# Making x by VectorE block transposes and on-chip DMAs, and a denser preparation of batch 0, in a fused clustered-attention and snake-MLP kernel

## The chip, the cores and the metric

One core of one Trainium2 chip. The time is the device time of one execution in microseconds; a kernel's time is the median of several executions. The first three executions of the kernel before agree within 0.4%. A profile is one execution recorded instruction by instruction; its span (317.6 us before) is a little shorter than that execution's time (319.34 us).

## The reference, cut to what matters

```python
# q, k, v: (4 batches, 8 heads, 768, 64); centroids: (8 heads, 16 clusters, 64)
q_assign = argmax(q_n @ c_n.T); k_assign = argmax(k_n @ c_n.T)
scores = where(q_assign == k_assign, q @ k.T / 8, -1e9)
x = softmax(scores) @ v          # heads side by side: (3072, 512)
h = x @ w_in                     # w_in (512, 2048)
g = h + sin(alpha * h) ** 2 / (alpha + 1e-9)
return g @ w_out                 # w_out (2048, 512)
```

The kernel writes the cluster of each row as a one-hot of 16 beside its 64 dimensions, so that one matmul over 80 rows gives scores that are large only where the clusters agree.

## The kernel before

Two heads are a *pair*, four pairs a batch, sixteen pairs in all. A batch is 48 *attention steps* (12 a pair), then a *hidden phase*: 16 feature blocks through w_in, the snake function and w_out. What the attention phase has left free on TensorE is filled with output products of the batch before. In these traces each engine works in program order (one block transpose of VectorE below waits 14.1 us, and the PV sums behind it wait too), and so does the queue of SP, which issues most DMAs between SBUF tiles. To *issue* a DMA is to hand it over, here some 0.6 us of the issuing queue; it *lands* when its data have arrived. In the listings T is a pair's transposed q and k, QK the same with the one-hot rows below, xs the x of a pair, xq its block-transposed form and xT the transposed x that the hidden phase reads; S, M and OB are areas of PSUM. A step, and the parts that the change touches:

```python
def scores(i):     # TensorE: 768 columns into one of two PSUM areas
    ...
def expo(i):       # ScalarE: exp of the area into pT (bf16)
    ...
def pv(i):         # TensorE: 6 products of 65 columns, summed over 6 steps in the one bank OB
    ...
    if kt == NJ - 1:                       # the sums of one head are done
        nc.vector.reciprocal(out=rec, in_=o3[:, :, D : D + 1])
        nc.vector.tensor_tensor(out=s["xs"][:, :, h, :], in0=o3[:, :, 0:D], ...)

def x_T(m, bk=None):                       # x of pair m, transposed, for the hidden phase
    ...
    for j in range(NJ):
        nc.tensor.transpose(out=xt_ps[:, P * j : P * j + P], in_=xs[:, j, :, :], identity=ident_b)
    nc.vector.tensor_copy(out=xT[:, hp, :], in_=xt_ps[:, 0:S])

def prep_S(m):     # T of q and k for a later pair (from batch 2 on): 8 DMAs, issued by SP
    ...
def prep_asn(m, part=0, parts=1):          # cluster products, 4 f32 matmuls; batch 0: in two halves
    ...
def prep_hot(m, piece, W=HS):              # VectorE: block transpose, max, compare, transpose back
    ...
def prep_move(m):                          # one-hot rows to their place in QK: 4 DMAs, issued by SP
    ...

def hidden_mm(f, ar, k0, k1):              # kk is the pair within the batch
    for kk in range(k0, k1):
        ...
        nc.tensor.matmul(..., rhs=xT[:, kk, lo:hi], ...)
```

At the end of each batch's steps, `hidden_mm(0, A[0], 0, 3)` reads x of the first three pairs; the fourth is always made by `x_T` inside the hidden phase.

The softmax here doesn't subtract the row's maximum and nothing guards it: scores larger than these inputs give would overflow.

## Time and profile before

| | before |
|---|---|
| time, median of 3 | 319.07 us (318.28 to 319.48) |
| first scores of batches 0 to 3 | 11.75, 86.01, 157.93, 229.35 us |
| first hidden product that needs the third pair's x, batches 1 to 3 | 129.2, 200.5, 270.0 us |
| TensorE busy | 97% |

The second and third rows are starts in TensorE's timeline. In the page's 40 slices, each digit is TensorE's busy share in tenths, and in the second line the clock it was granted:

```profile
PE   8789999899999999999999999999999999999995
PEclk9999999999999999999999999999999999999999
```

There is no slice in which TensorE idles for long, so a change can gain mainly by taking instructions from TensorE.

### The profile page before, as it was taken

The numbers are of one execution on the slowest core, as the hardware profiler recorded it, in microseconds if no ns is written. First come the engines' busy times: TensorE is split into PE (matmuls) and PEld (weight loads), VectorE is DVE, ScalarE is ACT, GpSimd is POOL, SyncE is SP. The second block draws the span as 40 slices with busy tenths as digits, with TensorE's granted clock in tenths as the row PEclk, the third lists the DMA queues.
The fourth block names the chain that finished last, engine by engine and source line by source line (L and its number), as shares of the span: only waits on it lengthen the run. The fifth ranks groups of instructions, "written<-read, shape, count | busy, mean of one in ns | idle before, by whom it ended". The sixth has DMA issues, their size and how long they took to land.

```text
span 317.6 us, 7292 instructions
## 1 busy us (share of the span) xinstructions
PE 306.6 (97%) x2835; PEld 183.0 (58%) x2835; DVE 205.3 (65%) x362; ACT 241.3 (76%) x326; POOL 111.3 (35%) x174
## 2 busy tenths in 40 slices
PE   8789999899999999999999999999999999999995
PEld 3456766555556566555556566555556666555544
DVE  4567879577858676587858676587836322577821
ACT  5578979787679888787679888787679999688300
POOL 5857968507603555960004374530001000000000
PEclk9999999999999999999999999999999999999999
DMA  7535899998825656890025656520011000000031
GB/s 232 187 111 164 259 143 207 221 209 215 273 86 124 153 122 153 231 351 32 0 85 131 154 120 141 141 85 0 0 68 42 30 12 35 2 34 0 2 132 66
DMA packets 26242, 37.74 MB, mean 119 GB/s; under 512 B 3856, under 2 KB 20064, under 8 KB 26208
## 3 DMA queue, kind: packets, MB, share of 16 engines
q0 software_dynamic: 8704, 19.93, 24.7%
q1 hardware_dynamic: 17264, 17.30, 20.2%
q8 instruction: 22, 0.36, 0.5%
q14 instruction: 12, 0.10, 0.1%
q10 hardware_dynamic: 240, 0.06, 0.1%
HBM read 27.30 MB, written 6.29 MB: 106 GB/s over the span
## 4 chain that ended last, share of the span: by engine, by line
PE 86%; DVE 7%; ACT 2%; DMA 2%; issue 1%; SPq 0%; DVEq 0%; ACTq 0%
PE M L361 18%; PE S L390 16%; PE S L314 12%; PE OB L329 10%; PE M L390 8%; PE S L315 6%; PE OB L361 5%; PE M L213 4%; PE S L361 2%; DVE gT L410 2%; PE M L143 2%; PE M L353 1%; ACT s_sb L401 1%; DMA q<-in_q_dram 1%; DVE u_sb L408 1%
## 5 line engine op out<-in xcount | busy, mean ns | idle before, releaser
L320 ACT ACTIVATE pT<-S 128x768 bf16<-128x768 f32 x192 | 144.4, 810 | 21.5 <-PE S L315 20.2
L361 PE MATMUL M<-w_out_bf,gT 128*128 128x512 bf16 (+1 forms) x288 | 90.7, 373 | 0.3 <-DVE gT L410 0.3
L314 PE MATMUL S<-QK 80*128 80x512 bf16 x192 | 73.1, 381 | 2.5 <-DMA QK<-ohT 2.4
L390 PEld LDWEIGHTS <-w_in_bf 128*128 128x128 bf16 x512 | 49.6, 98 | 38.0 <-issue 1.8
L329 PEld LDWEIGHTS <-pT 128*128 128x128 bf16 x1152 | 55.8, 97 | 21.5 <-DVE xs L341 0.5
L390 PE MATMUL S<-xT,w_in_bf 128*128 128x512 bf16 x352 | 65.2, 326 | 1.0 <-DVE gT L410 0.8
L329 PE MATMUL OB<-VX,pT 128*128 128x65 bf16 x1152 | 60.7, 193 | 0.3 <-DVE xs L341 0.2
L190 POOL TENSOR_SCALAR QK<-T 64x384 bf16<-64x384 f32 x64 | 33.6, 525 | 69.3 <-DMA T<-Tq 63.3
L401 ACT ACTIVATE s_sb<-S,alpha_col 128x768 bf16<-128x768 f32 x44 | 39.3, 901 | 23.7 <-PE S L390 14.5
L361 PEld LDWEIGHTS <-gT 128*128 128x128 bf16 x400 | 39.0, 97 | 30.7 <-issue 5.5
L315 PE MATMUL S<-QK 80*128 80x256 bf16 x192 | 51.9, 270 | 0.0
L410 DVE SCALAR_TENSOR_TENSOR gT<-u_sb,ralpha,S 128x768 bf16<-128x768 bf16 x44 | 44.5, 1014 | 11.1 <-ACT u_sb L406 8.2
L185 POOL CAST QK<-T 64x768 bf16<-64x768 f32 x32 | 26.4, 825 | 12.9 <-DVE T L149 8.5
L390 PE MATMUL M<-xT,w_in_bf 128*128 128x512 bf16 (+1 forms) x160 | 29.9, 326 | 0.0
L408 DVE TENSOR_TENSOR u_sb<-s_sb 128x768 bf16<-128x768 bf16 x40 | 23.6, 590 | 7.9 <-ACT s_sb L401 7.9
L340 DVE RECIPROCAL rec<-OB 128x6 f32<-128x6 f32 x32 | 6.1, 192 | 34.1 <-PE OB L329 34.1
L315 PEld LDWEIGHTS <-QK 80*128 80x128 bf16 x192 | 18.9, 98 | 15.2 <-issue 1.1
L410 DVE SCALAR_TENSOR_TENSOR gT<-u_sb,ralpha,M 128x512 bf16<-128x512 bf16 (+1 forms) x40 | 22.8, 611 | 6.4 <-ACT u_sb L406 6.0
L401 ACT ACTIVATE s_sb<-M,alpha_col 128x512 bf16<-128x512 f32 (+1 forms) x40 | 20.9, 574 | 7.2 <-PE M L390 7.2
L361 PE MATMUL OB<-w_out_bf,gT 128*128 128x512 bf16 (+1 forms) x80 | 26.2, 358 | 0.0
L202 POOL CAST VX<-v 128x768 bf16<-128x768 f32 x16 | 13.5, 844 | 34.3 <-PE OB L329 33.4
L314 PEld LDWEIGHTS <-QK 80*128 80x128 bf16 x192 | 18.6, 97 | 10.2 <-issue 5.7
(79 smaller groups left out, 270.3 us busy)
## 6 DMA issues: line engine op xcount, KB each, us to landing
T<-Tq SPq DMA_DIRECT2D x64, 96.0 KB, 2.4
out_dram<-o_sb SPq DMA_DIRECT2D x23, 256.0 KB, 2.1
v<-in_v_dram POOLq DMA_DIRECT2D x14, 384.0 KB, 4.6
q<-in_q_dram POOLq DMA_DIRECT2D x13, 384.0 KB, 5.5
k<-in_k_dram POOLq DMA_DIRECT2D x13, 384.0 KB, 6.3
w_in_bf<-in_moe_w_in_dram POOLq DMA_DIRECT2D x4, 512.0 KB, 8.3
w_out_bf<-in_moe_w_out_dram POOLq DMA_DIRECT2D x4, 512.0 KB, 11.4
QK<-ohT SPq DMA_DIRECT2D x60, 24.0 KB, 3.2
```

Of the source, the lines that this page charges most:

```text
L185: nc.gpsimd.tensor_copy(out=QK[0:D, m % NQK, h, :, HS * par : HS * par + HS], in_=src)
L190: nc.gpsimd.tensor_scalar(out=QK[0:D, m % NQK, h, t].rearrange("c (n i a) -> c i n a", i=4, a=32)[:, 2 * par : 2 * par + 2], in0=src[:, t] ...
L202: nc.gpsimd.tensor_copy(out=VX[m % NVX][:, :, :, 0:D], in_=st[m]["v32"])
L314: nc.tensor.matmul(out=dst[:, 0:512], lhsT=lhsT, rhs=T[:, 0, 0:512], start=True, stop=True)
L315: nc.tensor.matmul(out=dst[:, 512:S], lhsT=lhsT, rhs=T[:, 0, 512:S], start=True, stop=True)
L320: nc.scalar.activation(out=pT, in_=area(i)[:, 0:S], func=ACTF.Exp, scale=escale)
L329: nc.tensor.matmul(out=o3[:, j, :], lhsT=pT[:, P * j : P * j + P], rhs=VX[m % NVX][:, h, jof(m // NHP, kt), :], start=(kt == 0 and j == 0) ...
L361: nc.tensor.matmul(out=bk[:, lo:hi], lhsT=gT[:, f, P * mt : P * mt + P], rhs=w_out_bf[:, f, lo:hi], start=(f == 0), stop=(f == NF - 1),)
L390: nc.tensor.matmul(out=ar[lo // 512][:, 0 : hi - lo] if isinstance(ar, tuple) else ar[:, lo:hi], lhsT=lhsT, rhs=xT[:, kk, lo:hi], start=(k ...
L401: nc.scalar.activation(out=s_sb[:, lo:hi], in_=src, func=ACTF.Sin, scale=alpha_col[:, f : f + 1])
L408: nc.vector.tensor_tensor(out=u_sb, in0=s_sb, in1=s_sb, op=ALU.mult)
L410: nc.vector.scalar_tensor_tensor(out=gT[:, f, lo:hi], in0=u_sb[:, lo:hi], scalar=ralpha[:, f : f + 1], in1=src, op0=ALU.mult, op1=ALU.add,)
```

## The change

Its intent is to relieve TensorE in two ways. (1) The x of the first three pairs of batches 1 to 3 is no longer transposed by TensorE. VectorE transposes it in blocks of 32x32, and sixteen DMAs put the blocks in their places. For this xT gets a blocked layout, which TensorE reads in runs of 32 elements. (2) In batch 0 the cluster products are made whole, in steps that have no PV; the one-hots are dense, so the transpose back has 384 columns instead of 768 and the rows take eight DMAs instead of four. Loads and transposes of batch 0 move to other steps.

```diff
+    def x_D(m):
+        s["xq"] = xqp.tile([P, S], BF16, tag="xq", ...)        # a pool of one buffer
+        nc.vector.transpose(out=s["xq"]..., in_=s["xs"].rearrange("p j h (e d) -> p (h e) j d", e=2))
+    def x_S(m):
+        for g in range(4):
+            for i in range(4):
+                nc.sync.dma_start(
+                    out=xT[32 * g : 32 * g + 32, hp, QS * i : QS * i + QS],
+                    in_=st[m]["xq"][32 * i : 32 * i + 32, g, :],
+                )
 ...
-                    rhs=xT[:, kk, lo:hi],
+                    rhs=xT[:, kk, :].rearrange("c (i j a) -> c j i a", i=4, j=NJ)[:, lo // P : hi // P],
 ...
-            at(STEPS * (m + 1) + 4, lambda m=m: x_T(m))
+            if m < NHP:
+                at((16, 29, 43)[m], lambda m=m: x_T(m))
+            else:
+                at(STEPS * (m + 1) + 5, lambda m=m: (x_D(m), x_S(m)))
 ...
+            nc.vector.tensor_tensor(out=s["oh"]..., op=ALU.is_equal)                    # dense, batch 0
+            nc.vector.transpose(out=s["ohT"][:, 0, :], in_=s["oh"])                     # 384 columns
+                for par in range(2):                                                   # in prep_move
+                    nc.sync.dma_start(out=QK[D : D + NHC, m % NQK, h, t, HS * par : HS * par + HS], ...)
 ...
-        (2, ((0, 2), (1, 6), (2, 7), (3, 8)), (11, 12), (7, 10)),
+        (2, ((0, 5), (1, 6), (2, 8), (3, 10)), 14, (7, 11)),
 ...      # the like for pairs 1 to 6; loads, alpha and two transposes of pair 7 moved
```

## The prediction

> **What bounds the kernel now.** I read the page first (busy shares, then the chain that ended last), then TensorE's timeline, then the queue of SP, which issues most of the on-chip transfers.
>
> ```profile
> PE 306.6 (97%) x2835; PEld 183.0 (58%) x2835; DVE 205.3 (65%) x362; ACT 241.3 (76%) x326; POOL 111.3 (35%) x174
> PE 86%; DVE 7%; ACT 2%; DMA 2%; issue 1%; SPq 0%; DVEq 0%; ACTq 0%
> ```
>
> TensorE is the bound: 97% busy and 86% of the chain. SP's queue has 0% of it, so today no issue time costs anything. Four batches follow one another: 48 attention steps (scores, exponential, PV), then a hidden phase of 16 feature blocks. First scores start at 11.75, 86.0, 157.9 and 229.35 us, and the first hidden products at 55.9, 128.68, 199.97 and 269.47 us. An ordinary step in batches 1 to 3 takes 0.73 us from one scores matmul to the next. A step with a transpose of x looks like this in TensorE's timeline:
>
> ```profile
> 102.15 0.38 PE L314 MATMUL S<-QK 80*128 80x512 bf16 x1
> ...
> 102.66 0.50 PE L353 MATMUL M<-ident_b,xs 128*128 128x128 bf16 x6
> 102.99 0.38 PE L361 MATMUL M<-w_out_bf,gT 128*128 128x512 bf16 x1
> 103.20 0.38 PE L314 MATMUL S<-QK 80*128 80x512 bf16 x1
> ```
>
> The six transposes hold TensorE from 102.66 to 102.99: 0.33 us, and the step is 1.05 us long instead of 0.73. That is what the change wants to take away, nine times. Now the queue that will get the work instead, by SP's timeline in batch 1 and by its two lines of code:
>
> ```profile
> 93.07 6.57 SPq L175 DMA_DIRECT2D T<-Tq  x8
> 99.74 0.55 SPq L375 DMA_DIRECT2D out_dram<-o_sb  x1
> 100.39 2.45 SPq L288 DMA_DIRECT2D QK<-ohT  x4
> 103.02 7.02 SPq L175 DMA_DIRECT2D T<-Tq  x8
> 110.14 2.45 SPq L288 DMA_DIRECT2D QK<-ohT  x4
> ```
>
> ```profile
> L288 SPq DMA_DIRECT2D QK<-ohT x60: 507/587/1742, 21.2 to 245.9; - x60
> L175 SPq DMA_DIRECT2D T<-Tq x64: 586/609/2039, 93.1 to 199.0; - x64
> ```
>
> The reader is to see that SP issues one DMA after another, 0.59 to 0.61 us each (0.61 to 0.65 from start to start), almost whatever its size: 24 KB for QK, 96 KB for T. A pair lasts 9.76 us (x transposes at steps 16 and 28), of which SP is already issuing 8 to 9.5 us in batch 1. There is no room for sixteen more.
>
> **What the Trainium skill says.** "DMA: Bandwidth & Descriptors", section "Issuing engines are not separate DMA queues", holds that spreading issues over engines only saves sequencer time, "usually small relative to the DMA itself". The trace agrees only in part: T lands 2.4 us after issue, so the issue of one is a quarter of that, but sixteen issues in a row are four times the landing. "SBUF — State Buffer", "The DMA setup-cost knee", gives every DMA a fixed cost of about 2 us that does not shrink with its size; the 2.4 us for T and 3.2 us for QK agree, so cutting x into 12 KB pieces saves nothing. The same page, "Door 1: The DMA port swizzle", says that reads cost extra only where consecutive accesses leave a 16-byte line; the new reads of x by TensorE are runs of 32 bf16, 64 bytes, so I give them no cost. No read of such a kind is in this trace. "TensorE: Matmul & The Clock Gate", "Part 1: The HAM clock gate", has TensorE at half clock after some 3.4 us of idleness, until it has been busy as long. The trace before shows full clock nearly throughout, since nothing idles so long.
>
> **The change, part by part.**
> *x by VectorE and DMA.* Removed from TensorE: 9 x 0.33 = 3.0 us, all on the bound. ScalarE's exponentials run at 0.73 us a step too, so I count 2.5 to 3 us. VectorE loses a 0.56 us copy and gets a block transpose of 128x768 bf16, for which the strided one-hot transpose of the same size is the measure (0.98 us): +0.42 us a pair, beside other work (VectorE is busy 30 of 42 us there). SP gets 16 DMAs per pair: 16 x 0.61 = 9.8 us, nine times.
> They stand in program order behind and ahead of the T and QK issues. Their buffer is single, so VectorE's next block transpose waits until the previous sixteen have landed, and VectorE runs in order. And the hidden phase's first products read x of the third pair. So I add up SP's queue, in the times of the trace before, to the landing of the third pair's x (T 8 x 0.68 = 5.5 us, QK 2.5, an output 0.6, landing 2.3):
> Batch 1: the queue starts on pair 7's one-hot rows at 100.4 (eight DMAs now, 4.9 us) and from there never runs dry: T 110.8, x 120.6, QK 123.1, output 123.7, T 129.2, x 139.0, QK 141.5, T 147.0, x 156.8, landed 159.1. Before, the hidden products began at 128.7, and the first 0.65 us of them need only earlier pairs: delay 159.1 - 129.3 = 30 us.
> Batch 2: T starts at 174.3 as before: 179.8, x 189.6, QK 192.1, output 192.7, T 198.2, x 208.0, QK 210.5, T 216.0, x 225.8, landed 228.1, against 200.6: 27.5 us.
> Batch 3 has no T to issue. Block transpose at step 17, done 246.9; x 256.7, landed 259.0; the next block transpose, due near 255, waits for it, 260.0; x 269.8, landed 272.1; third 273.1; x 282.9, landed 285.2, against 270.1: 15 us.
> Sum 72.5 us. Within this, VectorE's waits (about 10 us for the second pair) also halt the steps, since the PV sums wait for VectorE to empty their bank, but SP is the slower of the two, so they are not added.
> After each of the three long waits TensorE would start cold: an estimate from the 3.4 us of that page is 1.7 us each lost, about 5 us in all; I take 3 because some may be shorter.
> The 3 us of transposes saved lie ahead of a wait for SP and are worth nothing then.
>
> *Batch 0.* Cluster products whole: two halves cost 0.46 us each on TensorE (30.31 to 30.77), a whole one 0.78 (105.81 to 106.59): 0.14 saved, six times, 0.8 us. Half-width one-hot transposes: 0.97 to about 0.57 us on VectorE (the f32 one of 384 columns takes 0.58), six or seven times, 2.6 us beside other work; a strided comparison of 1.0 us becomes dense, 0.56. Two visible waits may go: TensorE's at 23.7 (1.03 us, for one-hot rows to land) as the rows are made some three steps earlier, and the one at 45.4 (1.0 us, VectorE late with T). Against it: two transposes more in the steps, QK issues twice as many (8 x 0.61 = 4.9 us a pair, period at least 5 us). I take 2 us gained of 43.45.
>
> Total: 319.1 - 2 + 72.5 + 3 = 392.6, rounded to 392.
>
> **The rivals.**
> *The issue is hidden, and the 3 + 2 us come through:* 314 us. It would need SP to issue x several times faster than QK and T. For it: the first loads of the run took only 0.39 to 0.47 us each. Against it: even 0.43 us makes 6.9 us of sixteen, SP would still be past its 9.8 us a pair, and the same sum gives 392 - 9 x 2.9 = 366. QK's fastest of 60 took 0.507.
> *A cost in TensorE's reads of x:* 512 hidden matmuls start 0.21 and 0.11 us apart, 82 us in all; were reading in runs of 32 slower by 10%, this adds 8 us. Nothing in this profile speaks for it; it would be lost where TensorE waits for x anyhow only in part.
> *VectorE becomes the bound in the steps,* by the single buffer: it is what SP's backlog looks like from TensorE, and in batch 3, where SP has time, it is a real link. It is in the sum already.
> *DMA traffic:* sixteen more transfers of 32 rows of 384 bytes, 0.2 MB per pair. Bytes are small, but loads from memory share the engines; SP's issues waited up to 2.0 us in batch 1. In the instruction listing each SP DMA waits for the one eight places before it to land, so slow landings would lengthen the queue: up to 5 us a batch, 405 in all.
>
> **Range and chances.** The one term that matters is nine times sixteen issues. At 0.50 us each the sum is 376, at 0.65 us 398; slow landings or slow reads add 5 to 12, a better batch 0 or less cold start takes 4 off. I give 370 to 410. Slower by over 2% has 0.95: only my being wrong about the issue time by a factor would undo it.
>
> **What the profile after would show.** Right: SP's queue with rows of 16 issues of about 9.8 us in batches 1 to 3, end to end; the first hidden products stalled by a DMA on x for some 10 us in batches 1 to 3, and VectorE's block transpose waiting for DMA by up to 10 us; the chain with a large SP or DMA share; steps with x at 0.73 us where nothing waits; the lower clock digit in a few slices; batch 0 about 2 us shorter. Wrong: x issues of 0.2 us or less, or hidden products slower per piece than 0.32 us for 768 columns, or the hidden phases starting at their old distance from the first scores (43, 42, 40 us).

## The result, and the profile after

The changed kernel takes **401.53 us** (median of 4, 400.42 to 403.24) against 318.67 us of the kernel before (4 runs): ratio 1.260, 95% interval 1.254 to 1.266. Here and below a ratio is the mean time of one kernel's fast runs over that of the other's of the same rounds, so not quite the ratio of the medians. Executions over 1.5% slower than the fastest of the same kernel are left out of the means. The result was correct. The page, answering to the lines shown of before:

```profile
PE 317.2 (80%) x2695; PEld 186.6 (47%) x2733; DVE 206.5 (52%) x364; ACT 240.8 (60%) x324; POOL 111.6 (28%) x174
...
PE   7989998999938150899999392359999986399996
...
PEclk9999999999997756699999777859999989579999
...
PE 49%; SPq 26%; ACT 8%; DMA 7%; DVE 5%; issue 4%; DVEq 0%; ACTq 0%
```

TensorE is 80% busy instead of 97%, with three holes, in each of which its clock also drops. The chain that ended last now runs for 26% of the span through SP's queue, which had 0%. SP's timeline in batch 1 (start, duration, what was issued, how many):

```profile
96.05 5.55 SPq L295 DMA_DIRECT2D QK<-ohT  x8
101.78 5.21 SPq L176 DMA_DIRECT2D T<-Tq  x8
107.10 10.84 SPq L385 DMA_DIRECT2D xT<-xq  x16
118.04 2.43 SPq L300 DMA_DIRECT2D QK<-ohT  x4
120.56 0.53 SPq L407 DMA_DIRECT2D out_dram<-o_sb  x1
121.27 5.20 SPq L176 DMA_DIRECT2D T<-Tq  x8
126.57 10.64 SPq L385 DMA_DIRECT2D xT<-xq  x16
137.31 2.91 SPq L300 DMA_DIRECT2D QK<-ohT  x4
140.39 6.21 SPq L176 DMA_DIRECT2D T<-Tq  x8
148.64 10.73 SPq L385 DMA_DIRECT2D xT<-xq  x16
```

From 96 to 159 us one row begins almost where the row above ends (the longest gap, 2.0 us, is before the last row): SP does nothing but issue. What this did to the others, by the list of who waited for whom (total us, times, longest), and at the end of batch 1 by TensorE's timeline:

```profile
PE S L422 <- DMA xT<-xq: 28.4, 3, 10.7
DVE xq L376 <- DMA xT<-xq: 27.5, 4, 9.8
DVE xq L376 <- DMA QK<-ohT: 22.8, 2, 14.1
PE M L214 <- DVE o_sb L404: 20.6, 2, 13.0
PE OB L341 <- DVE xs L353: 19.9, 4, 8.0
```

```profile
149.45 0.81 PE L422 MATMUL S<-xT,w_in_bf 128*128 128x512 bf16 x4
149.78 0.49 PE L422 MATMUL S<-xT,w_in_bf 128*128 128x512 bf16 x2
160.84 0.80 PE L422 MATMUL S<-xT,w_in_bf 128*128 128x512 bf16 x2 [10.57 <-DMA xT<-xq]
```

TensorE has done the products of pairs 4 and 5 and stands for 10.57 us until the x of pair 6, issued last at SP, has landed. VectorE stands before its next block transpose, and TensorE's PV and cluster products then before VectorE.

Between the landmarks the 81.1 us of the two spans divide as follows ("resume" is the first hidden product that needs the third pair's x; the prediction's column is its sum, with the 3 us for a cold clock spread evenly):

| stretch | before | after | change | predicted |
|---|---|---|---|---|
| start to first scores of batch 1 | 86.0 | 83.2 | -2.8 | -2 |
| batch 1: first scores to resume | 43.2 | 77.7 | +34.5 | +30 |
| to first scores of batch 2 | 28.8 | 31.1 | +2.3 | +1 |
| batch 2: first scores to resume | 42.5 | 71.7 | +29.2 | +27.5 |
| to first scores of batch 3 | 28.9 | 30.9 | +2.0 | +1 |
| batch 3: first scores to resume | 40.6 | 54.9 | +14.3 | +15 |
| to the end | 47.6 | 49.3 | +1.7 | +1 |
| sum | 317.6 | 398.7 | +81.1 | +73.5 |

### The profile page after: what moved, and what is told of

It is laid out like the page before. It is cut to its first block, busy times and chain, and to the rows that moved or that the text cites. A ratio compares the mean times of both kernels' runs of the same rounds, so it can differ in the third digit from the quotient of the medians.

```text
span 398.7 us, 7267 instructions
## 1 busy us (share of the span) xinstructions
PE 317.2 (80%) x2695; PEld 186.6 (47%) x2733; DVE 206.5 (52%) x364; ACT 240.8 (60%) x324; POOL 111.6 (28%) x174
## 4 chain that ended last, share of the span: by engine, by line
PE 49%; SPq 26%; ACT 8%; DMA 7%; DVE 5%; issue 4%; DVEq 0%; ACTq 0%
SPq L385 21%; PE S L422 13%; PE M L393 9%; ACT pT L332 7%; PE M L422 6%; PE S L326 5%; PE OB L341 3%; PE OB L393 3%; SPq L176 3%; DMA xT<-xq 3%; PE M L214 2%; DMA T<-Tq 2%; PE S L327 2%; SPq L300 2%; PE S L393 2%
## 5 line engine op out<-in xcount | busy, mean ns | idle before, releaser
L422 PE MATMUL S<-xT,w_in_bf 128*128 128x512 bf16 x352 | 70.2, 341 | 30.0 <-DMA xT<-xq 28.4
L393 PE MATMUL M<-w_out_bf,gT 128*128 128x512 bf16 (+1 forms) x258 | 81.8, 380 | 0.5
L341 PEld LDWEIGHTS <-pT 128*128 128x128 bf16 x1152 | 60.2, 102 | 44.6 <-issue 25.1
L341 PE MATMUL OB<-VX,pT 128*128 128x65 bf16 x1152 | 64.9, 200 | 19.9 <-DVE xs L353 19.9
L326 PE MATMUL S<-QK 80*128 80x512 bf16 x192 | 76.4, 398 | 3.7 <-DMA QK<-ohT 1.3
L435 ACT ACTIVATE s_sb<-S,alpha_col 128x768 bf16<-128x768 f32 x44 | 39.3, 900 | 59.9 <-PE S L422 50.8
L393 PEld LDWEIGHTS <-gT 128*128 128x128 bf16 x400 | 39.3, 98 | 31.9 <-issue 6.7
L327 PE MATMUL S<-QK 80*128 80x256 bf16 x192 | 53.8, 280 | 0.0
L376 DVE STREAM_TRANSPOSE xq<-xs 128x768 bf16<-128x768 bf16 x9 | 8.7, 969 | 50.4 <-DMA xT<-xq 27.5
L422 PE MATMUL M<-xT,w_in_bf 128*128 128x512 bf16 (+1 forms) x160 | 31.3, 335 | 0.1
L214 PE MATMUL M<-T,cnB 128*32 128x384 f32 x120 | 14.5, 545 | 20.6 <-DVE o_sb L404 20.6
L327 PEld LDWEIGHTS <-QK 80*128 80x128 bf16 x192 | 19.6, 102 | 17.6 <-issue 4.4
L203 POOL CAST VX<-v 128x768 bf16<-128x768 f32 x16 | 13.6, 852 | 49.6 <-PE OB L341 48.7
L444 DVE SCALAR_TENSOR_TENSOR gT<-u_sb,ralpha,M 128x512 bf16<-128x512 bf16 (+1 forms) x40 | 22.8, 611 | 6.3 <-ACT u_sb L440 5.8
```

The source lines that it names most:

```text
L326: nc.tensor.matmul(out=dst[:, 0:512], lhsT=lhsT, rhs=T[:, 0, 0:512], start=True, stop=True)
L327: nc.tensor.matmul(out=dst[:, 512:S], lhsT=lhsT, rhs=T[:, 0, 512:S], start=True, stop=True)
L341: nc.tensor.matmul(out=o3[:, j, :], lhsT=pT[:, P * j : P * j + P], rhs=VX[m % NVX][:, h, jof(m // NHP, kt), :], start=(kt == 0 and j == 0) ...
L393: nc.tensor.matmul(out=bk[:, lo:hi], lhsT=gT[:, f, P * mt : P * mt + P], rhs=w_out_bf[:, f, lo:hi], start=(f == 0), stop=(f == NF - 1),)
L422: nc.tensor.matmul(out=ar[lo // 512][:, 0 : hi - lo] if isinstance(ar, tuple) else ar[:, lo:hi], lhsT=lhsT, rhs=xT[:, kk, :].rearrange("c ...
L435: nc.scalar.activation(out=s_sb[:, lo:hi], in_=src, func=ACTF.Sin, scale=alpha_col[:, f : f + 1])
```

## The experiments

The theory: SP's serial issue, some 0.6 us for each of sixteen DMAs a pair, is the loss. Rivals: the bytes or the number of transfers; VectorE's wait for its single buffer; TensorE's reads in runs of 32; an interference of the two parts. Every run had a correct result except the two that are wrong.

### One part alone

**x by TensorE again**, the rest of the change kept:

```diff
-            if m < NHP:
-                at((16, 29, 43)[m], lambda m=m: x_T(m))
-            else:
-                at(STEPS * (m + 1) + 5, lambda m=m: (x_D(m), x_S(m)))
+            at((16, 29, 43)[m] if m < NHP else STEPS * (m + 1) + 5, lambda m=m: x_T(m))
```

> The changed kernel with the x of its nine pairs made by TensorE again (into the same blocked layout), the rest of the change kept. Theory (SP's issue queue is the whole loss): the 81 us go, and batch 0 keeps the 2.8 us that the changed kernel's trace shows ahead of batch 1 (first scores at 83.18 instead of 86.01 us): 315 to 317 us. Rival (part of the loss lies in TensorE's reads of x in runs of 32): hidden products slower than 0.32 us for 768 columns, and 320 us or more.

Measured: 316.97 us (316.68 to 319.18, 6 runs), ratio to the kernel before 0.995 (0.992 to 0.999). All of the loss is gone, so it lay in the path of x.

**x by DMA alone**, batch 0 as in the kernel before (the diff is the x part of the change, nothing else):

> The kernel before with only the x of nine pairs changed to VectorE blocks and DMAs (batch 0 as before). Theory: the same SP queue as in the changed kernel, except that pair 7 issues four QK transfers instead of eight in batch 1 (2.5 us less) and batch 0 is 2.8 us longer: 400 to 406 us. If the two parts of the change interfered, this would be far from that.

Measured: 401.81 us (399.87 to 404.07, 4 runs), ratio 1.260. No interference of the two parts shows. Where batch 0's gain goes is not shown: in the two traces batch 1 begins 2.1 us later here (85.25 instead of 83.18 us), its stretch up to the resume is 0.8 us shorter, with four QK issues of pair 7 fewer in the crowded queue, and the rest is within the spread of the times.

### What of the sixteen DMAs costs: their number, their bytes, or the one queue

**Half the bytes, as many issues** (wrong):

```diff
-                    out=xT[32 * g : 32 * g + 32, hp, QS * i : QS * i + QS],
-                    in_=st[m]["xq"][32 * i : 32 * i + 32, g, :],
+                    out=xT[32 * g : 32 * g + 32, hp, QS * i : QS * i + QS // 2],
+                    in_=st[m]["xq"][32 * i : 32 * i + 32, g, 0 : QS // 2],
```

> The changed kernel with all sixteen x transfers per pair at half length (192 instead of 384 bytes a row), a wrong result on purpose. Theory (the number of issues counts): 399 to 403 us. Rival (bytes or traffic count): half of the x transfer time goes and the time falls by 10 us or more.

**The same half of the bytes in half as many issues** (wrong):

```diff
-            for i in range(4):
+            for i in range(2):
```

> The changed kernel with eight full-length x transfers per pair instead of sixteen, a wrong result on purpose: the same bytes as e5_half_bytes in half as many issues. Theory: 8 x 0.634 = 5.1 us less of SP's queue for each of nine pairs, on the path in nearly all: about 46 us less, 352 to 362 us. Rival (bytes): the same as e5_half_bytes.

Measured: 403.41 us with half the bytes, 0.4 us above the range expected, and 359.30 us with half the issues (one run each, so of unknown state). The bytes are the same in both; 72 issues fewer are worth 44.1 us, on average 0.61 us each. The issue rows (least, median, longest duration in ns) of the changed kernel, then of the run with half the bytes, are alike:

```profile
L385 SPq DMA_DIRECT2D xT<-xq x144: 507/589/1540, 107.1 to 347.4; - x144
```

```profile
L385 SPq DMA_DIRECT2D xT<-xq x144: 507/589/1589, 108.2 to 350.2; - x144
```

A row of 192 bytes costs the queue what a row of 384 does, and the traffic itself is not what TensorE waits for.

**All sixteen transfers, half of them issued from GpSimd's queue**:

```diff
-                nc.sync.dma_start(
+                (nc.sync if i % 2 else nc.gpsimd).dma_start(
```

> The changed kernel with eight of the sixteen x issues of each pair moved from SP to GpSimd's queue; all transfers are made and the result is right. Theory (serial issue on one queue): SP has 5.1 us less per pair, as in e6_half_issues; GpSimd pays about 8 x 0.75 = 6 us per pair beside its casts (its DMA instructions took 0.72 to 0.77 us before), which may delay casts a little: 352 to 372 us. Rival (the sixteen transfers themselves, their landing or VectorE's part): no change from 401 us.

Measured: 357.11 us (353.13 to 359.71, 4 runs), correct. The slowest of the four counts as a slow run; the fast three have a median of 356.56 us and the ratio 1.115 (1.106 to 1.123). All transfers are made, and 45 us go. Its issue rows on the two queues:

```profile
L385 POOL DMA_DIRECT2D xT<-xq x72: 496/496/582, 101.5 to 303.2; - x72
L385 SPq DMA_DIRECT2D xT<-xq x72: 507/588/1292, 108.3 to 303.7; - x72
```

GpSimd issued each in 0.50 us, not in the 0.75 us that I had taken from its larger loads; its total busy time rose from 111.6 to 146.9 us. So it is the serial queue. Even with half of the issues SP has some 5.2 us of T, 5.0 of x and 2.4 of QK for a pair, 12.6 us against a pair's 9.4 us of steps in batches 1 and 2. Of the 38 us of the loss that remain, 18.4 and 13.8 us lie there, up to the resume, and 1.8 us in batch 3, which has no T.

### VectorE's single buffer

**Two buffers for the block-transposed x** (the space comes from writing one scratch tile into another):

```diff
-    xqp = ctx.enter_context(tc.tile_pool(name="xqp", bufs=1))
+    xqp = ctx.enter_context(tc.tile_pool(name="xqp", bufs=2))
```

> The changed kernel with two buffers for the block-transposed x, so VectorE need not wait for the sixteen transfers of the pair before. Theory (SP's issues bind): TensorE reaches the hidden phases sooner and waits there longer; only batch 3, where the block transpose's wait holds SP back, gains, about 5 us: 393 to 399 us. Rival (VectorE's waits bind, 50 us of them in the trace): about 355 us.

Measured: 396.09 us (395.74 to 396.96, 4 runs), ratio 1.243 (1.240 to 1.245) against 1.260: 5.4 us gained, in the traces 4.0 us of it in batch 3, where the expectation placed it. In its list of waits VectorE's wait for the x transfers (27.5 us) is no longer there, nor is most of the one put down to QK (3.7 us left of 22.8), and TensorE waits longer for x:

```profile
PE S L422 <- DMA xT<-xq: 48.7, 4, 17.6
```

Taking VectorE's wait away moved the waiting to TensorE (28.4 to 48.7 us before the hidden products) instead of removing it. The wait that looked largest on VectorE was a consequence of the queue.

### TensorE's reads, and what batch 0's part is worth

**The plain layout**: as the first experiment, with xT laid out as in the kernel before:

```diff
-                    rhs=xT[:, kk, :].rearrange("c (i j a) -> c j i a", i=4, j=NJ)[:, lo // P : hi // P],
+                    rhs=xT[:, kk, lo:hi],
```

> As e1_x_by_pe, but with x in the plain layout of the kernel before: only batch 0's part of the change is left. Theory: reads in runs of 32 cost nothing, so this is within 0.3 us of e1_x_by_pe, about 316 us. Rival: if the runs cost 1% of the 82 us of hidden products, e1_x_by_pe is 0.8 us slower than this.

Measured: 316.86 us (315.90 to 318.49, 6 runs), ratio 0.994 (0.990 to 0.997), as with the runs. The groups of hidden products (busy us, mean ns of one), first with runs of 32, then plain:

```profile
L422 PE MATMUL S<-xT,w_in_bf 128*128 128x512 bf16 x176 | 59.8, 379 | 1.6 <-DVE gT L444 1.4
L422 PE MATMUL S<-xT,w_in_bf 128*128 128x256 bf16 x176 | 48.0, 272 | 0.0
```

```profile
L422 PE MATMUL S<-xT,w_in_bf 128*128 128x512 bf16 x170 | 58.1, 379 | 1.5 <-DVE gT L442 1.4
L422 PE MATMUL S<-xT,w_in_bf 128*128 128x256 bf16 x176 | 48.0, 272 | 0.3
```

379 and 272 ns in both (six records are missing from the second trace): reading in runs of 32 is free here.

**Full-width one-hots** on top of that, with four QK issues a pair instead of eight:

```diff
-        dense = m < NPE and W == HS
+        dense = False
 # and the full-width transpose and the four moves of the kernel before
```

> As e7_plain_layout, with the full-width one-hots and their full-width transposes of the kernel before, and so half as many QK issues in batch 0. If batch 0's gain comes from placing the whole products in steps without PV and from the earlier schedule, this keeps nearly all of it: 316 to 317 us. If it comes from the shorter VectorE work, this falls back to 318 us or more.

Measured: 317.88 us (316.66 to 319.11, 6 runs), ratio 0.997 (0.993 to 0.9997). The interval overlaps with that of the plain layout, so the times don't decide it. In the traces batch 0's steps, from first to last scores, take 41.8 us with full-width one-hots and 42.0 without: in these two executions nothing on the path came from the narrower transposes. The gain then lies in the whole cluster products and the earlier schedule, which were not tried apart.

### A version that uses the DMAs only where the queue has room

**Two pairs of batch 3 by DMA**, all else by TensorE, two buffers:

```diff
+            if m in (12, 13):
+                at(STEPS * (m + 1) + 5, lambda m=m: (x_D(m), x_S(m)))
+            else:
+                at((16, 29, 43)[m] if m < NHP else STEPS * (m + 1) + 5, lambda m=m: x_T(m))
```

> The changed kernel with x by DMA only for the first two pairs of batch 3, where SP has no T to issue, with two buffers, and by TensorE for all others. Theory: both transfers hide (10.3 us of issues in 31 and 19 steps of 0.73 us), and TensorE saves 2 x 0.33 us: 0.6 us faster than e1_x_by_pe, about 315.5 us. Rival: the x issues delay something else in batch 3 and nothing is gained.

> e8_two_pairs_by_dma once more, so that it shares chip and rounds with e10_xt_a_step_earlier: 316.9 us again, 0.7 us above e10.

Measured: 316.90 us (315.76 to 317.44, 6 runs), ratio 0.992 (0.989 to 0.995), and a second time 317.12 us (315.41 to 319.56), 0.994 (0.991 to 0.997). It beats the kernel before, but misses the 315.5 us expected, and a gain over x by TensorE is below what the times resolve. The trace shows why. SP's rows in batch 3, and TensorE's first wait after the steps:

```profile
239.18 2.41 SPq L300 DMA_DIRECT2D QK<-ohT  x4
241.95 10.47 SPq L385 DMA_DIRECT2D xT<-xq  x16
252.52 0.53 SPq L407 DMA_DIRECT2D out_dram<-o_sb  x1
253.16 11.24 SPq L385 DMA_DIRECT2D xT<-xq  x16
```

```profile
267.77 0.81 PE L422 MATMUL S<-xT,w_in_bf 128*128 128x512 bf16 x4 [1.18 <-issue]
```

The issues hide: steps 17 and 29 of batch 3 take 0.72 to 0.73 us instead of 1.06, its 48 steps 39.3 us instead of 40.0, and the last issue is out at 264.4 us, as the steps end (last scores at 265.4). The last landing does not hide: it comes at 267.58 us, and TensorE stands 1.18 us before the products of that pair. The profile puts this down to "issue" here; in e10's trace the same wait, 1.19 us, is put down to x, and in e11's there is none. From batch 3's first scores to the end the traces take 89.4 us (e8) and 88.1 us (e11), against 88.7 with x by TensorE: whether these two transfers gain anything is not shown.

**Its transposes a step earlier**, as the kernel before has them:

```diff
-                at((16, 29, 43)[m] if m < NHP else STEPS * (m + 1) + 5, lambda m=m: x_T(m))
+                at((16, 29, 43)[m] if m < NHP else STEPS * (m + 1) + 4, lambda m=m: x_T(m))
```

> As e8_two_pairs_by_dma, with TensorE's transposes of batches 1 to 3 back in the step in which the kernel before has them (one step earlier). In e8's trace the last of them, in batch 3, is followed by a wait of 0.65 us of an output product for VectorE's copy of x out of the same bank (the step takes 1.87 us); the kernel before has no such wait. Theory: that wait goes and nothing else changes: 0.7 us faster than e8, about 316 us by the median and 0.989 to 0.992 of the kernel before. Rival: the bank is taken by another group and nothing is gained.

Measured: 317.04 us (316.63 to 321.10, 6 runs), ratio 0.995 (0.991 to 0.999): no gain shown. In the trace the wait did go (the step takes 1.06 us instead of 1.87, and batch 3's steps 38.6 us instead of 39.3), but these 0.7 us drown in the spread of the new batch 0, whose steps took between 41.3 and 43.5 us in the profiled executions of the kernels that have it. The granted clock has a part in this spread: in the two longest (e1 and e11) it stands at half for 3.4 us near 25 us, and nothing of the gain is left in these steps. Of the 36 executions in the six runs near 317 us (e1, e7 to e11), the ten whose mean clock is 0.995 or less average 318.8 us, the other 26 average 316.8; of 36 executions of the kernel before, one has such a clock.

## Why the prediction was right

**The mechanism and the range held.** 401.5 us lies within 370 to 410, 9.5 us above the 392 predicted, and each named sign is in the trace: rows of sixteen issues end to end, three waits of hidden products for x (7.1 to 10.7 us), VectorE's block transpose waiting up to 14 us, steps with x at 0.72 us, the lower clock digit, SP in the chain. Its sums hold, but for small slips: 392.6 was rounded down, and three batches of 5 us more make 407, not 405.

**The size of an issue.** The prediction took 0.61 us from the QK rows, whatever the bytes. Measured: 0.589 us, and 0.633 from start to start (the pitch); that half the bytes change nothing and half the issues give 42 us is the direct proof.

**Where the 8 us between 73.5 and 81.1 lie** (the times differ by 9.5 us, since the span is one run):
- *SP's queue in batch 1*, predicted from 100.4 to 159.1, 58.7 us, took from 96.05 to 160.84, 64.8. A row of sixteen took 10.6 to 10.8 us, not 9.8, because the pitch was 0.633 us and the first issue in each was 0.5 to 0.7 us longer; and the third x began 8.3 us after the start of the T ahead of it, where 5.5 were counted. SP's list of waits shows 2.0 us there for a T to land, and inside that row of T one issue begins at 144.08 us, just as the QK transfer eight places before it has landed (144.06), and T's landings took up to 8.9 us beside loads from memory (GpSimd issues eight of q and k from 134 to 140 us). The prediction named slow landings as a rival, up to 5 us a batch; in batch 1 it came true, in batches 2 and 3 hardly.
- *The cold clock* was put at 3 us in all and cost about 6: the stretches after the three waits, which hold nearly the same work as before, are 2.3, 2.0 and 1.7 us longer, and the clock is at half for 5.0, 4.6 and 4.2 us after the resume. The estimate of 1.7 us each, from the 3.4 us of the Trainium skill's "TensorE: Matmul & The Clock Gate", "Part 1: The HAM clock gate", was nearer than the 3 us chosen, and still short: the half clock lasted longer than those 3.4 us.
- *Batches 2 and 3* were right to 1.7 us, and *batch 0*, put at 2 us, gained 2.8 in the trace.

**One step of batch 0 was wrong.** The wait for the one-hot rows before pair 1's scores was to go. It grew from 1.03 to 1.29 us. The rows are issued 3.9 us earlier (17.3 instead of 21.2 us), but in the chain one then takes 4.2 us to land (1.9 for the two that counted before), beside loads that the change also makes earlier (DMA busy share from 16 to 24 us: 0.84 instead of 0.36). This reading of it is an argument from the two traces; no run tried the old load steps with the new rows. The other wait, at 45.4 us, did go; it was 0.61 us of TensorE's products, and the 1.0 us of the prediction is the wait of their weight load.

**What stays open.** VectorE's wait of 14.1 us ahead of batch 1's third x is put down to QK's landing by the profile. That cannot be: the block transpose began at 142.49 us, and that QK transfer landed at 144.06. The last of the sixteen x transfers before it landed at 142.11 us (the slowest took 5.7 us), which fits the single buffer. Why landings were that slow there is not shown by any run; the loads beside them are an argument from the trace.

## What to carry to other kernels

Before moving work from a busy engine to DMAs, add up the issuing queue as you would an engine: number of DMAs times the pitch of its rows in the trace, against the time in which they must be out. Here sixteen small DMAs of 0.63 us replaced 0.33 us of TensorE, on a queue that was already issuing for 8.6 us of a pair's 9.8 in batch 1 although the chain gave it 0%. Where the queue was empty, in batch 3, the issues of two pairs hid, and only their last landing still held TensorE up, by 1.2 us in two of three traces. And a wait on an engine (here VectorE's buffer) may only be the queue seen from another place: take it away and see whether the total moves.

## What the Trainium skill lacked or had wrong

- "DMA: Bandwidth & Descriptors", "Issuing engines are not separate DMA queues": that spreading issues over engines only saves a sequencer time that is usually small misleads for many small DMAs. Moving half of the x issues from SP to GpSimd took 45 us off 401.5. Another page, "Perfetto Trace Analysis", "DMA Optimizations", says that balancing DMAs over the engines may help where descriptor generation is the bottleneck; it fits, and the first page lacks it.
- The same page, "Anatomy of one DMA — SWDGE (gpsimd) path", puts sequencer dispatch at about 50 ns and descriptor generation at "small, variable". The rows show 0.50 us an issue on GpSimd, far more than that dispatch. On SP, which that section does not treat, they show 0.59 us (pitch 0.633 us), the same for 192 and 384 bytes a row. The pages give parts of an issue's time; a queue's pitch by engine stands on none.
- "PSUM — Partial Sum Buffer", "Specifications", says that any non-contiguous access pattern slows matmuls significantly. TensorE's bf16 transposes that write PSUM in runs of 32 elements took 219 ns on average in e1_x_by_pe and started 56 ns apart, the same as contiguous ones in e7_plain_layout.
